# Attention, SoLU and softplus layers in one kernel: outputs of the split pairs made turned round, a TensorE subtraction for eight pairs, and a new order

## The chip, the cores and the metric

The kernel runs on one core of a Trainium2 chip. The metric is the time of one execution on the device in microseconds (us); the median of three runs of the kernel before is 711.85 us, from 709.94 to 712.74. A core has a TensorE for matmuls (PE in the profile, its weight loads PEld), VectorE (DVE), ScalarE (ACT), GpSimd (POOL) and SyncE (SP), which issues the DMAs; each engine works through its own list in order, and semaphores tie the lists together.

## The reference

Windowed attention (32 keys for the first four heads; every fourth of 128 for the last four), a layer with SoLU and layer norm, and a layer with softplus. Batch 4, 8 heads, 576 tokens, head size 64; 2304 tokens of 512 features for what follows.

```python
scores = scale * np.matmul(q, k.transpose(0, 1, 3, 2))
scores = np.where(masks[None, :, :, :], scores, -1000000000.0)
scores = scores - np.max(scores, axis=-1, keepdims=True)
attn = np.exp(scores)
attn = attn / (np.sum(attn, axis=-1, keepdims=True) + 1e-09)
x = np.matmul(attn, v)            # then tokens by 512 features

h = x @ w_in                      # 512 -> 1024
e = np.exp(h - np.max(h, axis=-1, keepdims=True))
solu = h * e / (np.sum(e, axis=-1, keepdims=True) + 1e-09)
mu = np.mean(solu, axis=-1, keepdims=True)
var = np.mean((solu - mu) ** 2, axis=-1, keepdims=True)
y = ((solu - mu) / np.sqrt(var + 1e-06) * g_ln) @ w_out     # 1024 -> 512

h2 = y @ w2_in                    # 512 -> 2048
g = np.maximum(h2, 0.0) + np.log1p(np.exp(-np.abs(h2)))
out = g @ w2_out                  # 2048 -> 512
```

## The kernel before

Large products are made from fp16 numbers: every fp32 operand is split into a high half and a low half (what the high half left over), and three products (high by high, high by low, low by high) add up in the accumulator. So each operand costs a conversion (high) and a subtraction (low).

**Attention.** Seven pairs of blocks for each batch, 28 in all; a block is 80 or 96 query rows, four heads, and 80 to 128 keys. The first ten pairs run in whole fp32 (`pair32`, `block32`), since TensorE has time early on. The other 18 (`pair`, `block`, line 1205) run on fp16 halves, and these 36 blocks are what the change is about. One of them goes like this: eight score matmuls; a masked maximum on VectorE; the exponential on ScalarE; the conversion to the high half `p` and the subtraction for the low half; a DMA that turns both over into `pT`; twelve matmuls of probabilities times values (`values`, line 1242), with `pT` as the stationary operand and 65 columns of `v` moving, of which the 65th is ones and yields the softmax sum. Then VectorE adds the epsilon to the sum, inverts it, scales the outputs into `xf` (or ScalarE does), splits these into `x`, and a DMA turns them over into `xr`, a ring of 768 tokens that holds the first layer's operand. The dilated heads go by way of `xd` and a reordering copy on ScalarE.

**Layers.** `m1` is the first layer's first product, for 18 tiles of 128 tokens (matmuls `ps_w<-W,xr`); `y` its second (`bank<-lnT,W`). The second layer goes in nine groups of 256 tokens: `h` (`bank<-y,W`), softplus, and `o` (`ps_w<-W,g`). The weights are scaled and split on VectorE and ScalarE as well, the second layer's in four quarters of its hidden width; the first two groups follow quarter by quarter as the weights come. `s1i` is the scale of the first weight, which needs the whole of it loaded.

**Order.** All work is first listed in a plan (class `Plan`, line 63) with an estimated cost for each engine that may do it. `order` (line 149) plays the plan through as events: each engine takes the ready piece that is due earliest, where the due times are the numbers of `TABLE` in tenths of a microsecond, one for each piece. Where TensorE has nothing in that play before 400 us, a filler is put into its list (line 263): a matmul of an identity matrix by itself into a free bank, 512 columns (`bank<-eye`, `ps_w<-eye`), whose result nobody reads. The list is fixed when the kernel is built. On the chip every engine runs its list in that order, and fillers run whether TensorE would have been idle or not. All recorded operations carry the lines of small helpers: 654 for a matmul, 660 for a TensorE transpose, 636 for ScalarE, 640, 642, 645, 648, 651 and 672 for VectorE, 663 and 666 for DMAs.

Of the kernel before, what the change touches and what calls it, by code (L numbers as in the profile page):

```python
# [20 lines left out]
DIL = 4  # L21
# [44 lines left out]
class Plan:  # L66
# [50 lines left out]

    def pace(self, now, us, cols):

        per = cols / us  # L120
        while True:
            w = int(now / self.WIN + 1e-9)
            while len(self.acts) <= w + 1:
                self.acts.append(0.0)
                self.fast.append(False)
            if w and not self.known[-1] >= w:
                for x in range(self.known[-1] + 1, w + 1):
                    self.fast[x] = self.acts[x - 1] >= self.KEEP
                    self.known.append(x)
            speed = 1.0 if self.fast[w] else 0.5  # L130
            left = (w + 1) * self.WIN - now
# [5 lines left out]
            now = (w + 1) * self.WIN  # L137
# [11 lines left out]
    def order(self):  # L149
# [18 lines left out]
        self.acts, self.fast, self.known, self.dense = [0.0], [False], [0], []  # L168
# [6 lines left out]
        while events:  # L175
# [120 lines left out]
def kernel(  # L296
# [35 lines left out]
    XL_PE = 0  # L332
# [640 lines left out]
    def pair(n):  # L973
# [62 lines left out]
        def vpart(s):  # L1036
            return v2.t[:kr, s, :, 0:D]
# [605 lines left out]
```

## Time and profile before

| | |
|---|---|
| median of three runs | 711.85 us |
| profiled execution, its own time | 712.54 us |
| its span in the trace | 710.8 us |
| mean granted TensorE clock | 0.983 of full speed |
| TensorE busy | 688.7 us, 97% |
| VectorE busy | 512.8 us, 72% |
| ScalarE busy | 440.1 us, 62% |
| DMA moved | 89.82 MB |

Busy shares are averages over stretches that differ. The kernel has a front, in which weights are converted and attention begins, and a long remainder of products; which engine is full has to be read for each stretch. The time from one group's start to the next one's start on TensorE says what a group costs there, since matmuls overlap and their recorded durations hold a pipeline's length.

### The profile page before, as it was taken

The numbers are of one execution on the slowest core, as the hardware profiler recorded it, in microseconds if no ns is written. First come the engines' busy times: TensorE is split into PE (matmuls) and PEld (weight loads), VectorE is DVE, ScalarE is ACT, GpSimd is POOL, SyncE is SP. The second block draws the span as 40 slices with busy tenths as digits, with TensorE's granted clock in tenths as the row PEclk, the third lists the DMA queues.
The fourth block names the chain that finished last, engine by engine and source line by source line (L and its number), as shares of the span: only waits on it lengthen the run. The fifth ranks groups of instructions, "written<-read, shape, count | busy, mean of one in ns | idle before, by whom it ended". The sixth has DMA issues, their size and how long they took to land.

```text
span 710.8 us, 14269 instructions
## 1 busy us (share of the span) xinstructions
PE 688.7 (97%) x5319; PEld 474.9 (67%) x5319; DVE 512.8 (72%) x1562; ACT 440.1 (62%) x909; POOL 3.5 (0%) x22
## 2 busy tenths in 40 slices
PE   6999797999999999999999999999999999999997
PEld 3665554867765577777765767677765677578853
DVE  4699999999999959958989989989555214411032
ACT  5588998889999478767787768749353102011110
POOL 1000000000000000000000000000000000000000
PEclk9799889999999999999999999999999999999999
DMA  9977886479966458979787786543110003000001
GB/s 265 243 210 232 260 229 174 134 159 194 226 115 149 138 165 198 237 134 166 143 163 133 136 166 124 109 93 71 42 35 26 1 1 90 1 1 1 1 30 60
DMA packets 186774, 89.82 MB, mean 126 GB/s; under 512 B 157000, under 2 KB 174416, under 8 KB 186704
## 3 DMA queue, kind: packets, MB, share of 16 engines
q1 hardware_dynamic: 186704, 88.90, 54.0%
q8 instruction: 42, 0.69, 0.4%
q14 instruction: 28, 0.23, 0.1%
HBM read 54.53 MB, written 4.72 MB: 83 GB/s over the span
## 4 chain that ended last, share of the span: by engine, by line
PE 70%; DVE 19%; DMA 4%; ACT 4%; issue 2%; SPq 0%; DVEq 0%; ACTq 0%
PE bank L654 37%; PE ps_w L654 32%; DVE W L645 3%; DVE E L645 2%; DVE st L1349 2%; DMA rk<-in_k_dram 1%; DVE s L1223 1%; DMA pT<-p 1%; DVE e L645 1%; DVE st L645 1%; PE bank L660 1%; DMA E<-in_k_dram 1%; DVE xr L648 1%; DVE hl L648 1%; ACT hl L636 1%
## 5 line engine op out<-in xcount | busy, mean ns | idle before, releaser
L654 PEld LDWEIGHTS <-W 128*128 128x128 f16 x2592 | 252.1, 98 | 36.6 <-issue 1.0
L654 PE MATMUL bank<-y,W 128*128 128x256 f16 x1728 | 196.2, 273 | 0.0
L654 PE MATMUL ps_w<-W,g 128*128 128x512 f16 x864 | 194.3, 379 | 0.0
L654 PEld LDWEIGHTS <-g 128*128 128x128 f16 x864 | 83.5, 98 | 92.0
L636 ACT ACTIVATE r<-bank,invC 128x512 f32<-128x512 f32 x72 | 49.0, 685 | 110.4 <-PE bank L654 79.6
L654 PE MATMUL ps_w<-W,xr 128*128 128x512 f16 x432 | 99.0, 382 | 0.1
L654 PE MATMUL bank<-lnT,W 128*128 128x256 f16 x864 | 97.4, 273 | 0.4 <-ACT r L636 0.4
L640 DVE TENSOR_SCALAR g<-r,KR 128x512 f16<-128x512 f32 x49 | 23.7, 484 | 86.9 <-PE ps_w L654 86.1
L654 PEld LDWEIGHTS <-xr 128*128 128x128 f16 x432 | 41.9, 100 | 46.9 <-issue 1.8
L645 DVE SCALAR_TENSOR_TENSOR g<-r,KR,g 128x512 f16<-128x512 f32 x72 | 53.8, 748 | 18.7 <-ACT g L636 15.4
L1611 ACT ACT_TABLE_LOAD x51 | 65.4, 1283 | 0.9
L636 ACT ACTIVATE s<-s 96x128 f32<-96x128 f32 (+3 forms) x144 | 43.7, 375 | 15.6 <-DVE s L642 9.3
L636 ACT ACTIVATE E<-E 128x768 f32<-128x768 f32 (+3 forms) x55 | 39.9, 729 | 13.3 <-DMA E<-in_v_dram 6.0
L1223 DVE CUSTOM_DVE_ANT_0 s<-bank,band,bsc 96x128 f32<-96x128 f32 (+3 forms) x144 | 39.0, 325 | 2.2 <-PE bank L654 1.2
L636 ACT ACTIVATE e<-ps_w,st,bsc 128x1024 f32<-128x1024 f32 x16 | 19.3, 1203 | 20.0 <-DVE st L640 14.5
L636 ACT ACTIVATE y<-bank 128x512 f16<-128x512 f32 x15 | 8.9, 591 | 33.7 <-PE bank L654 33.7
L645 DVE SCALAR_TENSOR_TENSOR E<-E 128x512 int32<-128x512 int32 x42 | 27.7, 684 | 0.0
L645 DVE SCALAR_TENSOR_TENSOR y<-bank,y 128x512 f16<-128x512 f32 x18 | 12.3, 686 | 21.3 <-ACT y L636 21.2
L1349 DVE TENSOR_REDUCE st<-ps_w 128x1 f32<-128x1024 f32 x18 | 22.0, 1222 | 7.8 <-PE ps_w L654 7.8
L654 PEld LDWEIGHTS <-eye 128*128 128x128 bf16 (+2 forms) x162 | 16.7, 110 | 14.5 <-issue 5.8
L654 PEld LDWEIGHTS <-pT 128*96 128x96 f16 (+3 forms) x432 | 22.6, 123 | 4.6 <-issue 1.0
L636 ACT ACTIVATE xf<-bank,rs 80x64 f32<-80x64 f32 (+1 forms) x92 | 21.0, 315 | 6.0 <-DVE rs L651 5.8
(197 smaller groups left out, 883.2 us busy)
## 6 DMA issues: line engine op xcount, KB each, us to landing
E<-in_moe_w_out_dram SPq DMA_DIRECT2D x18, 512.0 KB, 4.4
E<-in_moe_w_in_dram SPq DMA_DIRECT2D x16, 512.0 KB, 6.0
out_dram<-osb SPq DMA_DIRECT2D x18, 256.0 KB, 2.4
W<-in_moe_w_in_dram SPq DMA_DIRECT2D x8, 512.0 KB, 6.3
E<-in_v_dram SPq DMA_DIRECT2D x9, 384.0 KB, 4.2
E<-in_q_dram SPq DMA_DIRECT2D x9, 384.0 KB, 3.6
E<-in_k_dram SPq DMA_DIRECT2D x9, 384.0 KB, 4.0
W<-in_moe_w_out_dram SPq DMA_DIRECT2D x6, 512.0 KB, 5.4
```

The costliest lines, as they stand in the source:

```text
L636: pin(nc.scalar.activation(out=out, in_=in_, func=func, **kw))
L640: pin(nc.vector.tensor_scalar(out=out, in0=in0, scalar1=s1, scalar2=None, op0=op0))
L645: pin(nc.vector.scalar_tensor_tensor(out=out, in0=in0, scalar=s, in1=in1, op0=op0, op1=op1, **kw))
L648: pin(nc.vector.tensor_tensor(out=out, in0=a, in1=b, op=op))
L654: pin(nc.tensor.matmul(out, l, r, start=start, stop=stop))
L660: pin(nc.tensor.transpose(out, in_, eye32[:in_.shape[0], :in_.shape[0]]))
L1223: pin(nc.vector.tensor_tensor_reduce(out=sv()[:rows, h, :nk], in0=sb.t[:rows, h, :nk], in1=band[:rows, 48 - m:48 - m + nk], scale=sc[:rows ...
L1349: ({"DVE": (1.142, 0.14)}, lambda e: pin(nc.vector.tensor_reduce(out=col(0), in_=ph(), axis=AXX, op=ALU.max, negate=True)), [mb], [ps]),
L1611: pin(nc.scalar.preload_act_table_set(TABLES[tab]))
```

## The change

In `block`, the softmax sum now comes from the exponential itself (`accum_out`), and the probabilities are divided by it before they are split. The twelve matmuls swap their operands: 64 columns of `v` are stationary and the 80 or 96 rows of `pT` move, so that the outputs come out turned, feature by token. Two heads share a bank: the even one writes output partitions 0 to 63, the odd one 64 to 127, and the two alternate (`for g in range(2)`). High and low halves are then written straight into the ring, which takes away `xf` and `x` of these blocks, 36 turning DMAs, `xd`'s part and the reordering copies. The matmuls now wait for the ring's place (`wait`).

In `block32`, the low halves of the first eight pairs are made by TensorE: a matmul by a negative identity (`neg`) subtracts the high half in the accumulator (`xp`), and a copy takes the rest; before, VectorE subtracted.

The planner gets other constants (the windows by which it expects TensorE's speed, the price of a filler), some more orderings between pieces, and a new `TABLE`.

```diff
-    WIN, KEEP, HOLD = 3.4133, 3.0, 3.2
+    WIN, KEEP, HOLD = 3.4133, 3.25, 3.2
...
+    COLD = 10.0
...
+    def warm(self, w):
+        a = self.acts
+        return w >= 3 and a[w - 2] + a[w - 1] >= self.KEEP and a[w - 3] + a[w - 2] >= self.KEEP
...
-                idle_at["PE"] = self.pace(now, *self.FILL)
-                self.dense.append((now, idle_at["PE"], self.FILL[1]))
+                w = int(2 * now / self.WIN + 1e-9)
+                self.acts.extend([0.0] * (w + 2 - len(self.acts)))
+                self.acts[w] += self.FILL[1]
+                idle_at["PE"] = now + self.FILL[0] * (2 if now < self.COLD else 1)
...
-    XL_PE = 0
+    PV_US = 0.34
+    XL_PE = 8
...
     TABLE = (
-        170, 331, 228, 367, 475, 421, 396, 566, 185, 248, 154, 525, 248, 201, 208, 209, 237, 282, 204, 176, 278,
...
-    x2_pool = pool("x2", 1, [128, 2, HH, D], FP16)
-    xd_pool = Pool("xd", [])
...
-        if XL_PE:
+        if n < XL_PE:
             def residue(e):
                 for c0, cnt, r0, step in spans:
                     add(xt()[:, :, c0:c0 + cnt], neg, ring(0, r0, cnt, step))
...
-                act(sv()[:rows, h, :nk], sv()[:rows, h, :nk], ACTF.Exp, bias=nm()[:rows, h:h + 1])
+                act(sv()[:rows, h, :nk], sv()[:rows, h, :nk], ACTF.Exp, bias=nm()[:rows, h:h + 1], accum_out=mx()[:rows, h:h + 1])
...
-            for h in range(HH):
-                for x, (a, c) in enumerate(((0, 0), (0, 1), (1, 0))):
-                    mm(px[:rows, h, :], ptb.t[:nk, a * HH + h, :rows], v2.t[:nk, c, at[h], :], x == 0, x == 2)
-
-        pv = P.op(f"PV{name}", pe_cost(0.47), values, cols=0.6, after=[pt, *v_ops, *pv_ops[-1:]], uses=[ptb, v2, xb])
...
+            else:
+                tt(sv()[:rows, :, :nk], sv()[:rows, :, :nk], nm()[:rows].unsqueeze(2).broadcast_to([rows, HH, nk]), ALU.mult)
...
+            (TINY, lambda e: ts(nm()[:rows], mx()[:rows], 2.0 ** -14, 1e-9, ALU.mult, ALU.add)),
+            ({"DVE": (0.115, 0.14)}, lambda e: recip(nm()[:rows], nm()[:rows])),
+            ({**dve_cost(HH * nk), **act_cost(nk, ptr=1, k=4)}, times),
...
+            for c in range(2):
+                for x, (a, w) in enumerate(((0, 0), (1, 0), (0, 1))):
+                    for g in range(2):
+                        h = 2 * c + g
+                        mm(xt()[D * g:D * g + D, c, :rows], v2.t[:nk, w, at[h], :], ptb.t[:nk, a * HH + h, :rows], x == 0, x == 2)
+
+        pv = P.op(f"PV{name}", pe_cost(PV_US), values, cols=12e-3 * rows, after=[pt, *v_ops, *wait, *pv_ops[-1:]], uses=[ptb, v2, xb])
...
+                cast(e, ring(0, r0, cnt, step), xt()[:, :, c0:c0 + cnt], 2.0 ** -14)
...
+                stt(ring(1, r0, cnt, step), xt()[:, :, c0:c0 + cnt], 2.0 ** -14, ring(0, r0, cnt, step), ALU.mult, ALU.subtract)
```

**TensorE, the end of one block of probabilities times values before the last weight quarter.** In the kernel before (`pT` turned probabilities, `v` values, `xr` the ring):

```order
L654 LDWEIGHTS pT_105
L654 MATMUL bank_137<-v_111,pT_105 96x65
L654 LDWEIGHTS pT_105
L654 MATMUL bank_137<-v_111,pT_105 96x65
L654 LDWEIGHTS xr
L654 MATMUL ps_w_140<-W,xr 128x512
L654 LDWEIGHTS xr
L654 MATMUL ps_w_140<-W,xr 128x512
```

And in the changed kernel, at the corresponding place:

```order
L658 MATMUL bank_128<-pT_97,v_103 64x96
L658 LDWEIGHTS v_103
L658 MATMUL bank_128<-pT_97,v_103 64x96
L658 LDWEIGHTS v_103
L658 MATMUL bank_128<-pT_97,v_103 64x96
L658 LDWEIGHTS eye
L658 MATMUL bank_129<-eye 128x512
L658 LDWEIGHTS eye
```

`v` has become the stationary operand, and behind the block stand ten fillers (`eye`) where the first layer's matmuls followed.

**SP, the loads of the first weight.** Before (`W<-in_moe_w_in_dram` and `E<-in_moe_w_in_dram` are its pieces, eight in all; the last row here is the eighth):

```order
L663 DMA E<-in_moe_w_in_dram 128x1024 x2
L663 DMA W<-in_k_dram 128x4x64
L663 DMA W<-in_moe_w_in_dram 128x1024
L663 DMA W<-in_q_dram 96x4x64
L663 DMA W<-in_moe_w_in_dram 128x1024
```

Now, the rows that end with the eighth piece:

```order
L671 DMA W<-in_q_dram 96x4x64
L671 DMA W<-in_moe_w_out_dram 128x1024
L671 DMA rk_100<-in_k_dram 128x4x64
L671 DMA e_108<-in_moe_g_ln_dram 8x128
L671 DMA xd<-in_v_dram 128x4x64
L671 DMA rk_100<-in_k_dram 128x4x64
L671 DMA W<-in_k_dram 112x4x128
L671 DMA E<-in_moe_w_out_dram 128x1024
L671 DMA qk<-in_v_dram 128x4x64
L671 DMA E<-in_moe_w_out_dram 128x1024
L671 DMA xd<-in_v_dram 128x4x64
L671 DMA W<-in_moe_w_in_dram 128x1024
```

The eighth piece moved behind further loads of q, k and v, `g_ln`, and three pieces of `w_out`.

**VectorE, the middle of a split block.** Before (`s` scores and probabilities, `rs` the inverted sum, `xf` outputs, `x` their halves):

```order
L642 TENSOR_SCALAR s_113<-s_113 96x4
L640 TENSOR_SCALAR rs_166<-bank_137 96x4
L651 RECIPROCAL rs_166<-rs_166 96x4
L648 TENSOR_TENSOR xf_115<-bank_137,rs_166 96x256
L672 CAST x_116<-xf_115 96x256
L648 TENSOR_TENSOR x_116<-xf_115,x_116 96x256
```

Now (with weight conversions `E` and outputs `osb` between):

```order
L655 RECIPROCAL s_105<-s_105 96x4
L649 SCALAR_TENSOR_TENSOR E<-E 128x512
L649 SCALAR_TENSOR_TENSOR osb_123<-ps_w_131,invD,osb_123 128x512
L649 SCALAR_TENSOR_TENSOR osb_124<-ps_w_131,invD,osb_124 128x512
L680 CAST p_106<-s_104 96x512
L652 TENSOR_TENSOR s_105<-s_105 96x512
L652 TENSOR_TENSOR p_106<-s_104,p_106 96x512
L649 SCALAR_TENSOR_TENSOR xr<-bank_128,xr 128x2x72
```

The normalisation moved from the outputs to the probabilities, ahead of the split (`p`), and the ring's low half is made straight from the accumulator.

## Rows read from the trace of the kernel before

**Rows 1.** Windows: columns from to, length, busy (x instructions) of each engine, clock, DMA.
```profile
0.00:40.00 40.00, 33.38 (x216) 20.50 (x216) 24.24 (x63) 21.88 (x68) 3.52 (x22) 0.87 0.92 258
80.00:100.00 20.00, 16.72 (x97) 11.08 (x98) 19.46 (x47) 19.82 (x58) 0.00 (x0) 0.66 0.97 259
137.00:229.00 92.00, 91.65 (x737) 64.17 (x735) 91.36 (x291) 86.18 (x176) 0.00 (x0) 1.00 0.83 173
251.00:706.00 455.00, 453.40 (x3565) 318.86 (x3563) 280.69 (x875) 230.25 (x393) 0.00 (x0) 1.00 0.42 89
```

**Rows 2.** Timeline of TensorE around 136 us: start, length in us, operation.
```profile
135.17 0.82 PE L654 MATMUL bank<-qk,pT 128*96 128x65 f32 x8
135.82 1.24 PE L654 MATMUL ps_w<-eye 128*128 128x512 bf16 x5
136.90 1.36 PE L654 MATMUL bank<-y,W 128*128 128x256 f16 x11
```

**Rows 3.** Waits of TensorE from 136.9 us on: total, times, longest.
```profile
PE bank L654 <- ACT r L636: 0.4, 1, 0.4
...
PE bank L654 <- DMA pT<-p: 0.2, 1, 0.2
...
PE bank L654 <- DVE s L1223: 0.2, 1, 0.2
```

**Rows 4.** Timeline of TensorE around 245 us.
```profile
239.74 0.59 PE L654 MATMUL bank<-eye 128*128 128x512 bf16 x2
...
240.17 2.75 PE L654 MATMUL ps_w<-W,xr 128*128 128x512 f16 x12
...
245.49 5.40 PE L654 MATMUL bank<-y,W 128*128 128x256 f16 x48
...
250.73 0.38 PE L654 MATMUL bank<-eye 128*128 128x512 bf16 x1
```

**Rows 5.** Groups of VectorE by form: count, busy, mean ns, idle before.
```profile
L645 DVE SCALAR_TENSOR_TENSOR W<-W 128x512 int32<-128x512 int32 x22 | 15.1, 689 | 0.2
...
L645 DVE SCALAR_TENSOR_TENSOR W<-W,s2i 128x512 f16<-128x512 f32 x8 | 5.8, 744 | 0.0
...
L648 DVE TENSOR_TENSOR xr<-bank,xr 128x144 f16<-128x144 f32 x8 | 3.8, 474 | 0.6 <-ACT xr L636 0.5
...
L648 DVE TENSOR_TENSOR xr<-bank,xr 128x192 f16<-128x192 f32 x8 | 2.8, 352 | 0.2 <-ACT xr L636 0.2
```

**Rows 6.** DMA issues by kind, timeline of SP, and timeline of VectorE.
```profile
W<-in_moe_w_in_dram SPq DMA_DIRECT2D x8, 512.0 KB, 6.3
...
17.92 0.33 SPq L663 DMA_DIRECT2D W<-in_moe_w_in_dram  x1
...
39.75 0.15 DVE L640 TENSOR_SCALAR s1i<-tmp 128x1 f32<-128x1 f32 x1
```

**Rows 7.** Timeline of TensorE at two blocks.
```profile
181.79 0.69 PE L654 MATMUL bank<-v,pT 128*96 128x65 f16 x12
...
182.32 5.41 PE L654 MATMUL bank<-y,W 128*128 128x256 f16 x48
...
187.56 0.62 PE L654 MATMUL bank<-v,pT 112*80 112x65 f16 x12
...
188.01 0.57 PE L654 MATMUL bank<-kT,qT 128*80 128x112 f16 x8
...
188.47 1.80 PE L654 MATMUL bank<-y,W 128*128 128x256 f16 x15
```

**Rows 8.** Timeline of TensorE at an fp32 pair.
```profile
69.40 1.00 PE L654 MATMUL bank<-kT,qT 64*80 64x112 f32 x16
70.32 0.50 PE L660 MATMUL bank<-eye,rq 80*128 80x80 f32 x4
```

**Rows 9.** Groups of VectorE by form.
```profile
L648 DVE TENSOR_TENSOR p<-s,p 96x512 f16<-96x512 f32 x14 | 9.6, 683 | 0.1
...
L651 DVE RECIPROCAL rs<-rs 96x4 f32<-96x4 f32 x24 | 4.1, 169 | 0.1
```

More of the change, by code (lines that the diff above doesn't have):

```diff
@@ L116, in shy @@
         return self.SHY if e == "DVE" and len(o.opts) > 1 else 0.0
+    def warm(self, w):
+        a = self.acts
+        return w >= 3 and a[w - 2] + a[w - 1] >= self.KEEP and a[w - 3] + a[w - 2] >= self.KEEP
     def pace(self, now, us, cols):
         per = cols / us
+        part = self.WIN / 2
         while True:
-            w = int(now / self.WIN + 1e-9)
+            w = int(now / part + 1e-9)
             while len(self.acts) <= w + 1:
                 self.acts.append(0.0)
[L125 to L131, printed above, removed]
+            speed = 1.0 if self.warm(w) else 0.5
+            left = (w + 1) * part - now
             if us <= left * speed + 1e-9:
@@ L136, in pace @@
             us -= left * speed
-            now = (w + 1) * self.WIN
+            now = (w + 1) * part
     def short(self, now):
@@ L527 @@
     ams = [mem([128, 9], FP32, f"am{b}") for b in range(B)]
-    amw = [mem([128, 8], FP32, f"amw{i}") for i in range(2 + 2 * NQ)]
+    amw_mem = mem([128, 16 + 8 * NQ], FP32, "amw")
+    amw = [amw_mem[:, 0:8], amw_mem[:, 8:16], *(amw_mem[:, 16 + 4 * i:20 + 4 * i] for i in range(2 * NQ))]
     tmp = [mem([128, 8], FP32, f"tmp{i}") for i in range(4)]
@@ L589 @@
     xf_pool = pool("xf", 1, [128, HH, D], FP32)
-    x2_pool = pool("x2", 1, [128, 2, HH, D], FP16)
-    xd_pool = Pool("xd", [])
-    xd_pool.add(xd_mem.bitcast(FP16).rearrange("p (c r i) -> p c r i", c=4, r=DIL), opens=late)
-    dg_pool = pool("dg", 2 if LO_PE else 0, [128, 128], FP32)
+    dg_pool = Pool("dg", [quarter(3, 1152 + 128 * i, 128) for i in range(4)] if LO_PE else [])
     e_pool = pool("e", 1, [128, F1], FP32)
@@ L657, in add, with turned @@
         pin(nc.tensor.matmul(out, l, r, start=False, stop=True, skip_group_check=True))
-    def turned(out, in_):
-        pin(nc.tensor.transpose(out, in_, eye32[:in_.shape[0], :in_.shape[0]]))
+    def turned(out, in_, start=True):
+        one = eye32[:in_.shape[0], :in_.shape[0]]
+        if start:
+            pin(nc.tensor.transpose(out, in_, one))
+        else:
+            pin(nc.tensor.matmul(out, in_, one, is_transpose=True, start=False, stop=True, skip_group_check=True))
     def dma(out, in_):
@@ L724 @@
         nc.gpsimd.memset(s[0], 0.0)
-    for s in v_pool.slots:
-        nc.gpsimd.memset(s[0][:, 0, :, D:D + 1], 1.0)
-        nc.gpsimd.memset(s[0][:, 1, :, D:D + 1], 0.0)
     gb, gp = Buf(e_pool), Buf(ps_x)
@@ L1055, in pair, with landing @@
         )
-        x2s = []
         for o in range(2):
             at = [2 * h + o if kind else HH * o + h for h in range(HH)]
-            block(n, o, kind, b, i, half, rows, m[o], nk[o], sc, qt, kt, v2, at, [q_t, k_t], [v_h, v_l], due, x2s)
+            block(n, o, kind, b, i, half, rows, m[o], nk[o], sc, qt, kt, v2, at, [q_t, k_t], [v_h, v_l], due)
+    def landing(kind, b, i, o, half):
+        if kind == 0:
+            t0 = b * S + (2 * i + o) * RP
+            return [(0, RP, t0 % RING, 1)], token_wait(t0, t0 + RP), None
+        u = 2 * b + half
+        t0 = u * UNIT
+        off = (RD - UNIT // DIL) * half
+        spans, at = [], 0
+        while at < UNIT:
+            r0 = (t0 + at) % RING
+            cnt = min(UNIT - at, RING - r0)
+            spans.append((off + at // DIL, cnt // DIL, r0 + 2 * i + o, DIL))
+            at += cnt
+        return spans, token_wait(t0, t0 + UNIT), u
     def pair32(n, b, kind, i, half, rows, kr, m, nk, bufs, lds, due):
@@ L1095, in scores @@
                     mm(scored(o)[:rows, h, :nk[o]], qt.t[part, h, :rows], kt.t[part, h, :nk[o]], False, h == HH - 1)
-        qk_mm = P.op(f"QK{n}", pe_cost(0.05 + (4 + PAIRED * 16) * sum(nk) / 2400), scores, cols=4e-3 * sum(nk), after=turns, uses=[qt, kt, *sbs])
+        qk_mm = P.op(f"QK{n}", pe_cost(0.05 + (4 + PAIRED * 16) * sum(nk) / 2400), scores, cols=12e-3 * sum(nk), after=[*turns, *qk_ops[-1:]], uses=[qt, kt, *sbs])
+        qk_ops.append(qk_mm)
         for o in range(2):
@@ L1126, in block32 @@
         )
[L1127 to L1141 removed]
+        spans, wait, u = landing(kind, b, i, o, half)
         val = slice(1 - o, UW - o)
@@ L1148, in values @@
                 mm(px()[:rows, h, :], ptb.t[:nk, h, :rows], v3.t[:nk, h, UW * o:UW * (o + 1)], True, True)
-        pv = P.op(f"PV{name}", pe_cost(0.56), values, after=[cp, *v_ops, *wait, batch_ok[b]], uses=[ptb, v3, xb])
+        pv = P.op(f"PV{name}", pe_cost(0.56), values, cols=8e-3 * UW, after=[cp, *v_ops, *wait, batch_ok[b]], uses=[ptb, v3, xb])
         last32.append(pv)
@@ L1203, in block32, with block @@
             x_done.setdefault(u, []).append(xl)
-    def block(n, o, kind, b, i, half, rows, m, nk, sc, qt, kt, v2, at, qk_ops, v_ops, due, x2s):
+    def block(n, o, kind, b, i, half, rows, m, nk, sc, qt, kt, v2, at, turned_ops, v_ops, due):
         name = f"{n}.{o}"
         sb, s2, pb, ptb, xb = Buf(ps_s), Buf(s_pool), Buf(p_pool), Buf(pT_pool), Buf(ps_x)
-        xfb, x2b = Buf(xf_pool), Buf(x2_pool)
-        x2s.append(x2b)
         def scores(e):
@@ L1262, in block @@
-            ({"DVE": (0.115, 0.14)}, lambda e: recip(rr[:rows], rr[:rows])),
-            ({**dve_cost(256, x=1), **act_cost(64, ptr=1, psum=1, k=4)}, times, [], [xfb]),
-        ], after=[pv], uses=[xb])
-        xv = lambda: xfb.t
-        x_h = P.op(f"xh{name}", either(256), lambda e: cast(e, x2b.t[:rows, 0], xv()[:rows]), after=[nr], uses=[xfb, x2b])
-        x_l = P.op(f"xl{name}", dve_cost(256), lambda e: tt(x2b.t[:rows, 1], xv()[:rows], x2b.t[:rows, 0], ALU.subtract), after=[x_h], uses=[xfb, x2b])
@@ new lines, in block, with values @@
+        pt = P.op(f"pT{name}", dma_cost(1.35, 1.8), lambda e: dma_t(ptb.t[:, :, :rows], pb.t[:rows].rearrange("p a h c -> p (a h c)")), after=[p_l], uses=[pb, ptb], mv=moving(8 * rows, 256, 1.8))
+        spans, wait, u = landing(kind, b, i, o, half)
+        xt = lambda: xb.t[:, 0:2 * RP].rearrange("p (c r) -> p c r", c=2)
+        def values(e):
+            for c in range(2):
[3 more added lines that the diff above has]
+                        mm(xt()[D * g:D * g + D, c, :rows], v2.t[:nk, w, at[h], :], ptb.t[:nk, a * HH + h, :rows], x == 0, x == 2)
@@ new lines, in block, with ring, high, low @@
+        pv = P.op(f"PV{name}", pe_cost(PV_US), values, cols=12e-3 * rows, after=[pt, *v_ops, *wait, *pv_ops[-1:]], uses=[ptb, v2, xb])
+        pv_ops.append(pv)
+        def ring(a, r0, cnt, step):
+            return xr[:, kind, 2 * a:2 * a + 2, r0:r0 + (cnt - 1) * step + 1:step]
+        def high(e):
+            for c0, cnt, r0, step in spans:
+                cast(e, ring(0, r0, cnt, step), xt()[:, :, c0:c0 + cnt], 2.0 ** -14)
+        def low(e):
+            for c0, cnt, r0, step in spans:
+                stt(ring(1, r0, cnt, step), xt()[:, :, c0:c0 + cnt], 2.0 ** -14, ring(0, r0, cnt, step), ALU.mult, ALU.subtract)
@@ L1305 @@
+        k = len(spans)
+        n_x = 2 * sum(x[1] for x in spans) / k
+        xh = P.op(f"xh{name}", {**act_cost(n_x, psum=1, k=k), **dve_cost(n_x, x=1, k=k)}, high, after=[pv], uses=[xb])
+        xl = P.op(f"xl{name}", dve_cost(n_x, x=1, k=k), low, after=[xh], uses=[xb], due=due)
+        if kind == 0:
+            x_done[b, 0, 2 * i + o] = [xl]
+        else:
+            x_done.setdefault(u, []).append(xl)
     ln_bufs = {}
@@ L1464, in mlp2 @@
         add_prev = [None, None]
+        g_prev = g_last[-1] if not early else None
         for p in range(NP):
```

108 lines of the change are left out of this document (30 added, 78 removed), and 285 rows, old and new, of the table TABLE.

## Prediction

> **What bounds the kernel now.** I read the windows first, for which engine fills which stretch. VectorE is filled early: 19.46 of the 20 us from 80, in which TensorE's granted clock is 0.66 of full speed (the mean of its two levels, 1.2 and 2.4 GHz), and 91.36 of the 92 us from 137 to 229 [rows 1]. TensorE takes over when the second MLP can start: its first `h` matmuls begin at 136.90, right behind five filler matmuls [rows 2], and from there TensorE is busy 91.65 of the 92 us up to 229 and 453.40 of the 455 from 251 [rows 1]. The waits after 136.9 are five, 1.5 us in sum, the longest 0.4, the shortest 0.2 [rows 3]. So two clocks rule: before 137 us what VectorE must finish before the first `h`, after it how long TensorE's list is, fillers included. Third, the stretch to the last weight quarter: its first `h` is at 245.49 and the last filler at 250.73 [rows 4].
>
> The sum is made against the profiled execution, 712.54 us (span 710.8 and 1.74 around it), which is 0.7 above the median of 711.85.
>
> **First term: the start of the second MLP.** The second low half of `y` on VectorE is the gate of the first `h`. I counted VectorE's instructions up to it in both orders: 331 before, 313 after. The heavy ones that leave are four W<-W,s2i (744 ns each) and four W<-W (689) that now come later or go to ScalarE, and the subtractions that made the fp32 pairs' low halves: eight of 144 columns (474) and six of 192 (352) [rows 5], 11.6 us in sum; smaller ones (single conversions, 96-column subtractions, scale steps) make some 4 more. What is new ahead of it is near 11 us: weight conversions moved forward and to VectorE, four normalisations of outputs more, one pass over 1024 columns. Counted from an instruction's start to the next one's start, about 0.07 us less than its duration, the balance is 115.7 against 111.9: −3.8 us. VectorE is full there, so I take all of it: the first `h` at 133.1.
>
> Against it stands the load of the first weight. Its eighth piece is issued at 17.92 us and such pieces land after some 6 us [rows 6]; in the new order it stands twelve rows further back in SP's queue, with 9.6 MB ahead of it in place of 6.7. At 258 GB/s of the first 40 us [rows 1] that is 37 us in place of about 25, and its scale, at 39.75 now [rows 6], may be 3 to 5 us late. VectorE has other rows to do meanwhile (the count above holds them), so I charge nothing; uncovered it costs up to 5. Bounds of this term: −10 (VectorE's waits in the slow-clock stretch go as well) and +2.
>
> The 18 `xp` matmuls of the new low halves (two spans for some pairs) stand in this front, where TensorE waits for VectorE anyway; by the price of a filler each, 0.216 us, they are at most 3.9 us and cost nothing while VectorE sets the pace. ScalarE gets their copies, the sums of 144 exponentials and part of the normalising, and loses the six reordering copies and about half of the output scalings: some +9 us over the run, in an engine that is busy 86.18 of 92 us up to 229, without holding TensorE there, and 230.25 of 455 from 251 [rows 1].
>
> **Second term: fillers.** TensorE's list holds 142 fillers before and 217 after. Ahead of the first `h` there are 139 and 179; these lie under VectorE's work. Between the first `h` and the last quarter's first `h` it was 2 and is 38, with one more behind it before and none after: 35 more. Price: two fillers from 239.74 to 240.17, 0.216 us each [rows 4], so 7.6 us of TensorE's full list. A filler that stands where TensorE would wait is free; the five waits of 1.5 us in all [rows 3] show that about 0.8 of it may be: +6.8. Bounds: 0 (all stand where TensorE is held for the weights of the last quarter, VectorE's work for which has grown from 226.6 to 229.0 us by the same count), and +7.6.
>
> **Third term: probabilities times values.** 36 blocks of 12 matmuls. Before, 65 columns move: 20 blocks of 80 rows take 0.45 us (187.56 to 188.01), 16 of 96 rows 0.53 (181.79 to 182.32) [rows 7], 17.5 us in all. Now 80 or 96 columns move, with 64 columns stationary, alternately into the upper and the lower output partitions. If the halves run one behind the other, a column costs what the scores cost: eight matmuls of 112 columns in 0.46 us (188.01 to 188.47) [rows 7], 0.51 ns a column, so 0.49 and 0.59 us a block, 19.3 us: +1.8. If they run side by side, half of that, 9.7: −7.8. The trace has such a pair, though on row halves: sixteen records of fp32 score matmuls of 112 columns on 64 rows take from 69.40 to 70.32, 57 ns each, 0.51 ns a column, where eight records of 65 columns on whole rows take 0.65 us (135.17 to 135.82), 1.25 a column [rows 2, 8]. So row halves overlap. I take half the serial time and 0.1 us a block for entering and leaving the form, a choice between the ends that no row gives: 13.3 us, −4.2. Column halves aren't shown by any row, so both ends stay in the range.
>
> The row shows the half form running more than twice as fast per column. The Trainium skill, page "TensorEngine Tiling (Array Packing)", section "Key Properties", says that tiles work in parallel but that changing the tiling mode drains TensorE; the drain speaks against 36 blocks that each enter and leave the mode, and would be paid 72 times. No row here has the drain alone. The same skill's page "TensorE: Matmul & The Clock Gate", section "LDWEIGHTS (loading the stationary operand)", puts a load at its columns divided by 1.2 ns; by it 12 loads of 64 columns would alone take 0.64 us a block, an estimate, and the term would be +5.5. The trace disagrees with that as a spacing: load and matmul of 80 stationary columns follow each other every 38 ns [rows 7], where the rule gives 67.
>
> **The chain of a block.** Between exponential and fp16 split now stand a scalar step, a reciprocal (169 ns) and a multiplication over 512 columns, for which the nearest row is the p<-s,p subtraction, 683 ns [rows 9]: 1.0 us longer before the transposing DMA, and the single `p` buffer stays the same. Behind the matmuls the chain gets shorter: two steps to the ring in place of five steps and a DMA. VectorE's load per block is even. I take no wait from it, since chains run a block or more ahead and TensorE waited once, 0.2 us, for pT [rows 3]. SP loses 36 transposes; the queue isn't what is waited for after 41 us.
>
> Sum: −3.8 + 6.8 − 4.2 = −1.2 on 712.54, 711.3; less 0.7 for the median, 710.6 us.
>
> **Rivals.** (A) Faster: the halves overlap without a switching cost (−7.8 in place of −4.2) and the fillers keep the clock up where it stood at 0.66 for 20 us, 6.8 us of full speed [rows 1], so that the first `h` comes at about 127 (−10). With all fillers priced: 712.5 − 10 − 7.8 + 6.8 − 0.7 = 700.8; half of the front's gain gives 704. For it: TensorE's matmuls feed VectorE in that stretch. Against: VectorE has no idle time there to give back.
> (B) Slower: the longer chain arrives late at TensorE. The new list puts 9, 14 and 10 fillers right around blocks of probabilities times values: the order itself foresees TensorE without work there. Each block that isn't covered costs its 1.0 us; as queued work on TensorE stands behind the block in a fixed order, nothing fills it. It decides from five late blocks on (715.6); with eight, 710.6 + 8 = 718.6. For it: VectorE is full to 229, so each of the added steps queues. Against: 28 of the 36 blocks come after the last filler, where VectorE is busy 280.69 of 455 us [rows 1].
> (C) The change doesn't do what it says: the halves go serially, +1.8 in place of −4.2, and the time is 716.6.
>
> **Chances.** The forecast 0.5 (706 to 715), A 0.18, B 0.2, C 0.12. The measurement tells 0.5% from no change, that is below 708.3 or above 715.4. Of the forecast's half 0.15 lies below, 0.3 between, 0.05 above; A is below but for 0.02; B is above but for 0.04; C is split 0.04 to 0.08. Faster 0.31, same 0.40, slower 0.29. The range that leaves out a tenth on either side is 701 to 720.
>
> **What would show it.** The first `h` at 133 (right) or past 137 (load of the first weight or chain late). The blocks' slots on TensorE: 0.34 and 0.40 us if the halves overlap with a cost around them, 0.25 and 0.3 without, 0.5 and 0.6 if serial. The last quarter's first `h` within 3 us of 245.5 and TensorE busy over 99% behind it; waits on pT, or on a ring copy, of more than 3 us in sum speak for B. Wrong in principle would be a TensorE that waits after 260 us, or fillers that take over 0.3 us each because the clock is low.

## The result, and the profile after

The changed kernel takes 716.7 us (median) against 711.51 for the kernel before in the same comparison, a ratio of 1.0066 with an interval from 1.004 to 1.0092: slower by about 5 us. I had forecast 710.6 and a range up to 720; the time lies in the range, on the wrong side of the kernel before. One of its six executions took 1851.61 us, stands outside the ratio, and without it the median is 716.6. The profiled execution took 716.6 us, span 714.9, mean clock 0.994.

The windows of the changed kernel (from to, length, busy time of PE, PEld, DVE, ACT and POOL, clock, DMA share, GB/s), to hold against [rows 1]:

```profile
0.00:40.00 40.00, 34.81 (x267) 21.47 (x268) 25.81 (x62) 26.35 (x81) 3.37 (x18) 1.00 0.98 276
80.00:100.00 20.00, 15.92 (x109) 9.93 (x107) 19.35 (x57) 19.06 (x53) 0.00 (x0) 0.83 0.80 221
133.00:229.00 96.00, 94.00 (x743) 63.92 (x742) 93.64 (x293) 85.72 (x195) 0.00 (x0) 1.00 0.71 161
257.00:710.00 453.00, 451.94 (x3564) 311.69 (x3563) 275.65 (x854) 241.98 (x518) 0.00 (x0) 1.00 0.40 83
```

The clock is full over the first 40 us (0.87 before) and 0.83 in place of 0.66 from 80 to 100, and TensorE is busy nearly everywhere. A reader of these four lines would see a kernel that got better. Where the second layer begins on TensorE (start, length, operation), against [rows 2]:

```profile
131.74 0.60 PE L658 MATMUL ps_w<-eye 128*128 128x512 bf16 x2
132.17 1.55 PE L658 MATMUL bank<-qk,pT 96*96 96x65 f32 x16
133.56 2.78 PE L658 MATMUL bank<-y,W 128*128 128x256 f16 x24
```

The first `h` is at 133.56, 3.3 us earlier. Two blocks of probabilities times values, against [rows 7]; the next row's start ends the slot:

```profile
187.27 0.45 PE L658 MATMUL bank<-pT,v 128*64 128x96 f16 x12
187.65 0.61 PE L658 MATMUL bank<-y,W 128*128 128x256 f16 x4
...
205.80 0.41 PE L658 MATMUL bank<-pT,v 112*64 112x80 f16 x12
206.14 2.79 PE L658 MATMUL bank<-y,W 128*128 128x256 f16 x24
```

0.38 and 0.34 us a block, where it was 0.53 and 0.45. Now TensorE ahead of the last weight quarter, against [rows 4]; the last row is the quarter's first `h`:

```profile
222.76 0.41 PE L658 MATMUL bank<-pT,v 112*64 112x80 f16 x12
223.10 2.12 PE L658 MATMUL bank<-eye 128*128 128x512 bf16 x9
226.42 2.75 PE L658 MATMUL ps_w<-W,g 128*128 128x512 f16 x12 [1.20 <-DVE osb L649]
...
234.81 3.18 PE L658 MATMUL bank<-eye 128*128 128x512 bf16 x14
237.92 0.45 PE L658 MATMUL bank<-pT,v 128*64 128x96 f16 x12
238.30 2.33 PE L658 MATMUL bank<-eye 128*128 128x512 bf16 x10
240.65 7.93 PE L658 MATMUL ps_w<-W,xr 128*128 128x512 f16 x36
248.42 0.28 PE L658 MATMUL bank<-amw,ones 128*128 128x4 f32 x2
248.56 2.75 PE L658 MATMUL ps_w<-W,xr 128*128 128x512 f16 x12
251.15 0.59 PE L658 MATMUL bank<-eye 128*128 128x512 bf16 x2
251.58 0.60 PE L658 MATMUL bank<-y,W 128*128 128x256 f16 x4
```

It is at 251.58, 6.1 us later than before, behind 33 fillers in three places and two more just ahead of it. In that list `bank<-amw,ones` at 248.42 is the matmul that sums the squares of the last weight piece: the second weight's scale, without which the quarter's `h` is not let go in the plan. VectorE's steps from it to the scale, in the changed kernel:

```profile
248.74 0.16 DVE L846 TENSOR_REDUCE tmp<-bank 128x1 f32<-128x4 f32 x1 [1.17 <-PE bank L658]
248.93 0.15 DVE L644 TENSOR_SCALAR s2o<-tmp 128x1 f32<-128x1 f32 x1
...
250.79 0.15 DVE L649 SCALAR_TENSOR_TENSOR KR<-s2o,tmp 128x1 f32<-128x1 f32 x1
```

and the same steps in the kernel before:

```profile
243.08 0.16 DVE L840 TENSOR_REDUCE tmp<-bank 128x1 f32<-128x4 f32 x1 [0.16 <-PE bank L654]
243.28 0.15 DVE L640 TENSOR_SCALAR s2o<-tmp 128x1 f32<-128x1 f32 x1
...
245.02 0.15 DVE L645 SCALAR_TENSOR_TENSOR KR<-s2o,tmp 128x1 f32<-128x1 f32 x1
```

The scale is 5.7 us later, and in both kernels `h` starts within a us of `KR`. That does not make the scale what TensorE waits for: its matmul stands in TensorE's own list, straight behind 36 matmuls of the first layer, VectorE waits 1.17 us for it (0.16 before), and `h` follows behind twelve more matmuls and two fillers without a pause. The scale marks how late the stretch is. The account of the span, +4.1: first `h` −3.3; from there to the last quarter's first `h` 118.0 us in place of 108.6, +9.4; from there to the last matmul 458.1 in place of 459.9, −1.8; the tail −0.2.

The windows of the stretch that got longer, from the first `h` to the last quarter's, before and then now:

```profile
136.90:245.50 108.60, 108.25 (x824) 72.05 (x823) 107.04 (x339) 94.58 (x190) 0.00 (x0) 1.00 0.76 166
133.56:251.60 118.04, 116.02 (x863) 73.78 (x863) 113.11 (x352) 96.14 (x216) 0.00 (x0) 1.00 0.64 150
```

VectorE is 6.1 us busier in it (113.11 in place of 107.04) and idle for 3.4 us more (4.9 in place of 1.6): together the 9.4.

### The profile page after: what moved, and what is told of

The parts are those of the page before. It is cut to its first block, busy times and chain, and to the rows that moved or that the text cites. A ratio compares the mean times of both kernels' runs of the same rounds, so it can differ in the third digit from the quotient of the medians.

```text
span 714.9 us, 14467 instructions
## 1 busy us (share of the span) xinstructions
PE 696.0 (97%) x5412; PEld 468.9 (66%) x5412; DVE 511.7 (72%) x1536; ACT 452.5 (63%) x1056; POOL 3.4 (0%) x18
## 4 chain that ended last, share of the span: by engine, by line
PE 72%; DVE 12%; DMA 7%; ACT 6%; issue 2%; SPq 0%; DVEq 0%; ACTq 0%
PE bank L658 37%; PE ps_w L658 33%; DMA E<-in_moe_w_in_dram 2%; DMA lnT<-hl 2%; DVE E L649 2%; PE bank L666 2%; ACT E L640 1%; DVE W L649 1%; DMA pT<-p 1%; ACT W L640 1%; DVE s L1230 1%; DMA E<-in_moe_w_out_dram 1%; ACT hl L640 1%; ACT e L640 1%; DMA rk<-in_k_dram 1%
## 5 line engine op out<-in xcount | busy, mean ns | idle before, releaser
L658 PEld LDWEIGHTS <-W 128*128 128x128 f16 x2592 | 251.6, 98 | 35.4 <-issue 0.4
L640 ACT ACTIVATE s<-s 96x128 f32<-96x128 f32 (+3 forms) x156 | 57.4, 375 | 14.4 <-DVE s L646 12.1
L640 ACT ACTIVATE E<-E 128x768 f32<-128x768 f32 (+3 forms) x51 | 38.0, 745 | 16.4 <-DVE E L649 9.4
L1230 DVE CUSTOM_DVE_ANT_0 s<-bank,band,bsc 96x128 f32<-96x128 f32 (+3 forms) x144 | 39.0, 324 | 13.0 <-PE bank L658 12.8
L658 PEld LDWEIGHTS <-eye 128*128 128x128 bf16 (+2 forms) x237 | 23.1, 104 | 23.0 <-POOL eye L721 3.8
L640 ACT ACTIVATE xr<-bank 128x144 f16<-128x144 f32 (+2 forms) x76 | 26.8, 402 | 16.9 <-PE bank L658 14.0
L658 PE MATMUL ps_w<-eye 128*128 128x512 bf16 x131 | 36.1, 396 | 0.2 <-DVE e L649 0.2
L640 ACT ACTIVATION_READ_ACCUMULATOR s<-s 80x1 f32 (+1 forms) x144 | 26.9, 187 | 0.0
```

The costliest lines, as they stand in the source:

```text
L640: pin(nc.scalar.activation(out=out, in_=in_, func=func, **kw))
L658: pin(nc.tensor.matmul(out, l, r, start=start, stop=stop))
L1230: pin(nc.vector.tensor_tensor_reduce(out=sv()[:rows, h, :nk], in0=sb.t[:rows, h, :nk], in1=band[:rows, 48 - m:48 - m + nk], scale=sc[:rows ...
```

## The experiments

Theory 1: the fillers fill TensorE's list and cost their price. Theory 2: VectorE reaches the last scale later, TensorE must wait for it, and the fillers only stand in the wait. Beside it a question of the second kind: what the short blocks are due to. Times below are medians, with the ratio to the kernel before measured on the same chip and its interval; the starts are read from each run's timeline. The starts come from one profiled execution of each run and scatter by 1 to 1.5 us: experiment 3 only reorders the twelve matmuls of a block and has the last quarter at 250.6 where the changed kernel has 251.6, and experiment 1 changes nothing ahead of the first `h` and has it at 135.0 where the changed kernel has 133.6. The table holds, in us, the first `h`, the scale steps (`s2o<-tmp`) and the first `h` of the last quarter, and the stretch from there to the last matmul.

| run | first h | last scale | last quarter | behind it | ratio (interval) |
|---|---|---|---|---|---|
| before | 136.9 | 243.3 | 245.5 | 459.9 | 1 |
| changed | 133.6 | 248.9 | 251.6 | 458.1 | 1.0066 (1.004 to 1.0092) |
| 1, no late fillers | 135.0 | 253.6 | 255.8 | 457.2 | 1.0115 (1.0093 to 1.0136) |
| 2, no multiplication | 133.7 | 247.2 | 249.8 | 457.4 | 1.0047 (1.0027 to 1.0067) |
| 3, halves in turn | 133.7 | 248.0 | 250.6 | 459.1 | 1.0069 (1.0044 to 1.0093) |
| 4, multiplication on ScalarE | 133.0 | 249.3 | 252.0 | 459.2 | 1.0093 (1.0072 to 1.0115) |
| 8, low halves on VectorE | 135.5 | 249.8 | 252.5 | 456.8 | 1.007 (1.0048 to 1.0092) |
| 13, no block work early | 133.4 | 246.3 | 248.9 | 457.1 | 1.0035 (1.0017 to 1.0054) |
| 14, no sums early | 133.9 | 247.9 | 250.5 | 458.3 | 1.0057 (1.0037 to 1.0076) |
| 15, before, more on VectorE | 135.7 | 246.8 | 249.0 | 459.7 | 1.0064 (1.0036 to 1.0093) |

**1. The late fillers left out.**

```diff
+        late_part = late_part or isinstance(o, Op) and o.name == "h0.0"
+        if late_part and not isinstance(o, Op):
+            continue
```

Expected: 

> The changed kernel without the 38 fillers that stand after the first h matmul; the order of everything else is kept. Theory 1 (the fillers fill TensorE's list and cost their 0.216 us each): 8.2 us less, 708 to 709. Theory 2 (VectorE reaches the scale of the last weight quarter 5.7 us later, TensorE has to wait for it, and the fillers stand in that wait): the first h of the last quarter stays near 251, waits of 8 to 10 us appear in its place, and the time is 715 to 717.5.

Measured: 719.76 us, 3 us slower than with them. TensorE in the same stretch (idle time and its releaser in brackets), and the windows:

```profile
223.60 0.41 PE L658 MATMUL bank<-pT,v 112*64 112x80 f16 x12
226.71 4.44 PE L658 MATMUL ps_w<-W,g 128*128 128x512 f16 x12 [2.70 <-DVE osb L649]
...
239.79 0.45 PE L658 MATMUL bank<-pT,v 128*64 128x96 f16 x12 [2.85 <-DVE xr L649]
242.63 10.61 PE L658 MATMUL ps_w<-W,xr 128*128 128x512 f16 x36 [2.39 <-DVE osb L649]
```

```profile
220.00:240.00 20.00, 14.45 (x89) 6.55 (x89) 17.46 (x42) 10.05 (x27) 0.00 (x0) 0.91 0.40 104
240.00:260.00 20.00, 17.61 (x100) 9.47 (x95) 15.25 (x47) 10.67 (x21) 0.00 (x0) 0.83 0.41 132
```

Waits stand in the fillers' three places, 7.9 us in sum, for VectorE's output sums (`osb`) and a low half of the ring (`xr`). The granted clock falls there: the twelve matmuls behind the first wait take 4.44 us in place of 2.75, the 36 of the first layer behind the third 10.61 in place of 7.93. The last quarter starts 4.2 us later still, of which 1.4 is there at the first `h` already. Theory 1 falls: without the fillers TensorE waits in their place, and with them it keeps the clock. Theory 2 had waits of the right size, on the right engine and in the fillers' places, but not what is waited for, which is never the scale; and it missed the clock, 2 us above its range.

**2. The multiplication left out.**

```diff
-        o.fn(o.on)
+        if not (o.name.startswith("nr") and o.name.endswith("c") and int(o.name[2:].split(".")[0]) >= NF):
+            o.fn(o.on)
```

Expected: 

> The changed kernel with the multiplication of the probabilities by the inverted sum left out in the 36 split blocks (sum and reciprocal stay), so the outputs are not divided by the softmax sum; order kept, fillers too. Theory 1: TensorE's list is as long as before, 716 to 717. Theory 2: five of these passes (0.57 us each from start to start) leave VectorE ahead of the last quarter's scale, and the blocks' chains get shorter; the scale and the first h of the last quarter come 2 to 4 us earlier, 712.5 to 714.5.

Measured: 714.95 us. The last quarter starts 1.8 us earlier and the time is 1.8 lower. The direction is theory 2's, the size just short of what it had; but by experiment 3's trace the quarter is only 0.8 us earlier, and the intervals of the ratios overlap, so a gain is likely and not certain.

**3. Halves in turn.**

```diff
-                for x, (a, w) in enumerate(((0, 0), (1, 0), (0, 1))):
-                    for g in range(2):
-                        h = 2 * c + g
+                for g in range(2):
+                    h = 2 * c + g
+                    for x, (a, w) in enumerate(((0, 0), (1, 0), (0, 1))):
```

Expected: 

> The changed kernel with the twelve matmuls of a split block in the order head by head (three into the upper output half, then three into the lower) in place of alternating. If the alternation is what lets them run side by side, a block takes 0.49 and 0.59 us in place of 0.34 and 0.38; the 28 blocks behind the last quarter's start cost 5 us, 721 to 722 us. If the alternation doesn't matter, 716 to 717.5.

Measured: 716.48 us, ratio 1.0069 (1.0044 to 1.0093). The alternation does not matter; a miss for the first reading. Whether the short slots are real was then open, hence 5 to 7.

**4. Five multiplications on ScalarE.**

```diff
+        if isinstance(o, Op) and o.name in ("nr10.0c", "nr11.1c", "nr12.0c", "nr13.0c", "nr13.1c"):
+            o.on = "ACT"
```

Expected: 

> The changed kernel with five of the multiplications ahead of the last weight quarter's scale (blocks 10.0, 11.1, 12.0, 13.0, 13.1) on ScalarE in place of VectorE, same place in the order. Theory 1: no change, 716 to 717. Theory 2: VectorE is 2.9 us earlier at that scale, 713.5 to 715, unless ScalarE's four instructions for each (about 1.6 us) make the block's chain late, which would take part of it back.

Measured: 718.13 us; the last scale did not come earlier (249.3), and the remainder got 1.1 us longer. The remainder of experiment 3 is as long without such a cause (459.1), so the 1.1 is scatter. VectorE's relief was lost on ScalarE, which is 18.7 to 19.8 us busy of each 20 from 180 to 220 in the changed kernel: VectorE waits for it 4.7 us between 133 and 252 us, 0.6 in the changed kernel. So the proviso held, in full.

**5 to 7. Each block's matmuls five times**, in the changed kernel alternating, head by head, and in the kernel before.

```diff
+            for again in range(5):
                 for c in range(2):
                     for x, (a, w) in enumerate(((0, 0), (1, 0), (0, 1))):
```

Expected, alternating: 

> The changed kernel with the twelve matmuls of each split block issued five times over (the same result each time), halves alternating. If the slots in the trace (0.34 and 0.38 us) are what TensorE is held for, the four extra passes cost 4 x 0.35 us in each of the 28 blocks behind the last quarter's start, 39 us, and up to 51 with the eight ahead of it: 756 to 768. If the matmuls really take a column's time of the scores, 0.49 and 0.59, it is 60 to 77 us: 777 to 794.

Expected, head by head: 

> The same five passes, but head by head (three matmuls into the upper output half, then three into the lower). If a side-by-side run of the halves makes the short slots, it needs alternation, and this comes out 15 to 25 us above the alternating one. If the 64 columns of the stationary operand make them, the two are within 2 us.

Expected, the kernel before: 

> The kernel before with its twelve matmuls of each split block issued five times over. By its slots (0.45 and 0.53 us) the extra passes cost 4 x 0.49 us in 28 to 36 blocks, 55 to 71 us: 767 to 782. The difference to the alternating run of the changed kernel, per pass and block, is what the new form saves.

Measured: 746.85, 746.81 and 779.48 us, two executions of each. The 144 extra passes cost 30 us in either new form, 0.21 a pass, and 68 us in the old, 0.47. The new form came out below both of my numbers, since the first pass of a block is dearer than the next four (and of the 33.5 us by which the blocks' slots grew, some fell into TensorE's waits). The new form's timeline:

```profile
175.32 1.47 PE L658 MATMUL bank<-pT,v 128*64 128x96 f16 x60
176.72 0.50 PE L658 MATMUL bank<-y,W 128*128 128x256 f16 x3
```

and the old form's:

```profile
189.91 2.46 PE L654 MATMUL bank<-v,pT 112*80 112x65 f16 x60
192.20 0.57 PE L654 MATMUL bank<-kT,qT 128*80 128x112 f16 x8
```

Five passes of 96 columns take 1.40 us (175.32 to 176.72) where one takes 0.38: 0.255 for each further one, 21 ns a matmul, 0.22 ns a column, under half of the scores' 0.51 [rows 7]. So the short slots are real. Head by head is as fast, which by the expectation of that run speaks for the 64 stationary columns as the reason, and not for halves that need alternation. Whether two halves run side by side is not shown: no run puts all twelve matmuls into one half. Five passes of 80 columns take 1.20 us in the same trace, 0.215 for each further one. A block alone thus costs 0.12 us more than a further pass, of its 0.34 or 0.38; I put that down to entering and leaving the form. In the old form five passes take 2.29 us (189.91 to 192.20), 0.46 each, the first no dearer than the others.

**8. The low halves of the first eight pairs on VectorE again.**

```diff
-                    add(xt()[:, :, c0:c0 + cnt], neg, ring(0, r0, cnt, step))
+                return
...
-                    cast(e, ring(1, r0, cnt, step), xt()[:, :, c0:c0 + cnt])
+                    tt(ring(1, r0, cnt, step), xt()[:, :, c0:c0 + cnt], ring(0, r0, cnt, step), ALU.subtract)
```

Expected: 

> The changed kernel with the low halves of the first eight pairs subtracted on VectorE from the accumulator again, at the places where the copies stood, and without the 18 subtracting matmuls; all else in the same order. If VectorE's list sets the first h and the last quarter's scale, its 15 to 18 more instructions (0.27 to 0.4 us each) put both 4 to 5 us later, 719.5 to 721. If the front has slack, 716 to 717.5.

Measured: 716.75 us, no change that the intervals resolve. The first `h` is 1.9 us later, little more than the scatter, the last scale 0.9, and nothing of it is seen at the end. This part of the change is worth nothing that these runs can tell.

**9 to 11. The last two quarters' weight work pulled ahead in the built order**, by up to 6 and 3 us, and by 6 in the kernel before.

```diff
+    for x in [o for o in order if isinstance(o, Op) and o.name.startswith(("w2i2", "w2o2", "w2i3", "w2o3")) and o.on != "SP"]:
+        at = order.index(x)
+        to = at
+        while to and not clash(x, order[to - 1]) and (not isinstance(order[to - 1], Op) or order[to - 1].t0 > x.t0 - 6.0):
+            to -= 1
+        order.insert(to, order.pop(at))
```

Expected, 6 us: 

> The changed kernel with every instruction of the second layer's last two weight quarters (their conversions, squares, scales on VectorE, ScalarE and TensorE) pulled ahead of other work in the built order by up to 6 us of the plan, as far as what it reads and writes allows; nothing added or left out. Theory 2a (the place of these instructions in VectorE's list sets the last quarter's start): the scale and the first h of the last quarter come 3 to 5 us earlier, 712 to 714. Theory 2b (loads, squares and the scale matmul set it, VectorE waits then at these places): no change, 716 to 717.5, with VectorE's waits grown by as much. Theory 2c (the work pushed behind makes the blocks and o late): the quarter starts earlier, but TensorE waits elsewhere, 716 to 719.

Expected, 3 us: 

> As the one before, but pulled ahead by up to 3 us only. 2a: 1.5 to 3 us earlier, 714 to 715.5. 2b: no change. 2c: less of a delay elsewhere than with 6, 715.5 to 717.

Expected, the kernel before: 

> The kernel before with the same pull of up to 6 us. In it TensorE's list is full up to the last quarter's start (waits and fillers of 1 us there), so an earlier scale can give at most 1 us: 710.5 to 712; if the blocks are made late, 713 to 715.

Measured: 767.67, 742.86 and 761.82 us, 51, 26 and 50 us slower (the third against the kernel before): none of my theories had that. What VectorE waits for from 137 to 300 us in the first of them (total, times, longest):

```profile
DVE tmp L846 <- PE bank L658: 11.7, 4, 4.8
DVE E L646 <- DMA E<-in_moe_w_out_dram: 8.0, 3, 3.9
DVE st L1339 <- PE ps_w L658: 6.3, 1, 6.3
DVE E L646 <- DMA E<-in_moe_w_in_dram: 5.5, 3, 2.5
```

Pulled ahead, an instruction stands at the head of an in-order list before its load or its matmul is there, and all behind it wait. The chain to the scale is thus load, conversion, square, matmul, each on another engine with two load buffers, and VectorE's list is full in between: a chain and a full engine at once.

**12. `h` without the second weight's scale.**

```diff
-            need = [*w2_d[qd][0], w2_ok[qd]]
+            need = w2_d[qd][0]
...
-                lambda e, ps=ps, rb=rb, cq=cq: act(rb.t, ps.t, ACTF.Softplus, scale=invC[:, cq]), after=[hm], uses=[ps, rb], tab=2,
+                lambda e, ps=ps, rb=rb, cq=cq: act(rb.t, ps.t, ACTF.Softplus, scale=invC[:, cq]), after=[hm, *scaled_by], uses=[ps, rb], tab=2,
```

Expected: 

> The changed kernel in which a quarter's h matmuls wait for that quarter's first weight alone, and only the softplus behind them for the scale of the second weight (which is what it reads); the planner makes a new order from that. If the wait for the scale is what TensorE loses, h of the last quarter starts some 12 us earlier and up to two of them run ahead of the scale: 5 us less, 711.5 to 713. If other work is missing then in the same place (the first layer's tiles), 715 to 718.

Measured: 715.0 us, ratio 1.006 (1.0038 to 1.0082). The last quarter's first `h` moved to 234.6, the scale stayed at 250.6, and 26 fillers now stand in one row ahead of `y`: two `h` run ahead, then TensorE is without work again. The ratio is that of the changed kernel (1.006 and 1.0066): no gain, though `h` no longer stands behind the scale. The planner made a new order for it, so more than this differs.

**13 to 15. Less VectorE work, fewer ScalarE sums, and more VectorE work in the kernel before**, each in the pairs 10 to 13, which come ahead of the last quarter. 13 leaves out their normalising steps and low halves, 14 the sums.

```diff
+        if o.name.startswith(("nr10", "nr11", "nr12", "nr13", "xl10", "xl11", "xl12", "xl13")):
+            continue
```

```diff
-                act(sv()[:rows, h, :nk], sv()[:rows, h, :nk], ACTF.Exp, bias=nm()[:rows, h:h + 1], accum_out=mx()[:rows, h:h + 1])
+                act(sv()[:rows, h, :nk], sv()[:rows, h, :nk], ACTF.Exp, bias=nm()[:rows, h:h + 1], **({} if n < 14 else {"accum_out": mx()[:rows, h:h + 1]}))
...
-            (TINY, lambda e: ts(nm()[:rows], mx()[:rows], 2.0 ** -14, 1e-9, ALU.mult, ALU.add)),
+            (TINY, lambda e: ts(nm()[:rows], mx()[:rows], *((0.0, 1.0) if n < 14 else (2.0 ** -14, 1e-9)), ALU.mult, ALU.add)),
```

```diff
         o.fn(o.on)
+        if o.name.startswith(("pl10", "pl11", "pl12", "pl13")):
+            o.fn(o.on)
```

Expected, 13: 

> The changed kernel in which the four split pairs that come ahead of the last quarter's start (10 to 13) leave out VectorE's normalising steps (scalar step, reciprocal, multiplication) and the low half into the ring; three multiplications of ScalarE go too. Order and fillers kept. Some 7 us of VectorE's list ahead of the last scale. If VectorE's block work is the cause: the last scale 4 to 6 us earlier, near the 243 us of the kernel before, and the total 711 to 713. If loads or ScalarE set it: 715 to 717.

Expected, 14: 

> The changed kernel in which the exponentials of the pairs 10 to 13 don't read out their sums (32 of them, about 0.1 us of ScalarE each; the outputs of these pairs are not divided by the sum). If ScalarE sets the last quarter's start: 2 to 3 us earlier, 713.5 to 715. If VectorE does: 716 to 717.5.

Expected, 15: 

> The kernel before with the low half of the probabilities of the pairs 10 to 13 made twice (8 more passes of about 0.57 us on VectorE, same result), order kept. If VectorE's list ahead of the last scale is the bound: the scale and the last quarter's start 3 to 4.6 us later and the total 714.5 to 716.5, as in the changed kernel. If VectorE has slack there: 711 to 712.5.

Measured: 713.62, 715.75 and 715.44 us. The mirror, 15, came out as theory 2 had it: eight more passes, some 4.6 us of VectorE, put the last quarter of the kernel before 3.5 us later (4.8 counted from its first `h`) and the time 4 us up. 13 gives 2.7 us at the last quarter (1.7 by experiment 3's trace) and 3 in the time, less than I had expected. Its window from the first `h` to the last quarter says why:

```profile
133.40:248.90 115.50, 115.50 (x862) 73.77 (x862) 108.06 (x323) 92.81 (x204) 0.00 (x0) 1.00 0.66 154
```

VectorE has 5.0 us less to do than in the changed kernel, and TensorE is not idle for a moment. The fillers were kept, 38 in 8.5 us of this stretch, and with VectorE relieved they are the limit: more than TensorE's 2.0 us of idle time (118.04 less 116.02) could hardly be gained in 2, 13 or 14. 13 without fillers was not run.

14 has the last quarter at 250.5, which is where experiment 3 has it (250.6), and its ratio can't be told from the changed kernel's. No effect of ScalarE's sums is shown.

## Why the prediction was wrong

- First term, the first `h` 3.8 us earlier: right (3.3). The count of VectorE's instructions carried it. The late load of the first weight also came (`s1i` at 45.35 in place of 39.75) and was hidden, as charged. But I let this gain count to the end. Part of it was work put off: four `W<-W,s2i`, which the count takes out ahead of the first `h`, start between 133.97 and 138.55 now, 3.0 us of VectorE right behind it (rows below). Experiment 8 points the same way: 1.9 us lost ahead of the first `h` left nothing in the time that the intervals resolve.
- Third term, the blocks: the size was right, 17.7 us of slots down to 12.8, −4.9 where I had −4.2, and the cost around a block is 0.12 us, I had 0.1. The reason, halves side by side like the fp32 row halves, is not shown (5, 6). The prediction's other price, +5.5 if load time sets the spacing, is refuted by experiment 5, at 18 to 21 ns for a load and its matmul. Behind the last quarter's start, where TensorE is full, 28 blocks gave 3.8 us, of which 1.8 is left: from start to start, `h` and `o` take 1.7 and 0.8 us more there, in waits of at most 0.41.
- Second term, the fillers at +6.8: the step that failed, and with it "the last quarter's first `h` within 3 us of 245.5". I priced the fillers as added work on a full list, took that list for what bounds the stretch, and put TensorE's wait for VectorE at nothing. Experiment 1 shows the wait: without the fillers TensorE stands idle for 7.9 us in their three places, for `osb` and `xr`, and the quarter comes no earlier. The stretch is 9.4 us longer, as much as VectorE's 6.1 us of work and 3.4 of idle time more in it. That the two sums were not far apart hid the mistake: 6.8 of list against 9.4 of waiting. The price of a filler was fair, and where VectorE is relieved (13) the list with its fillers is the limit after all.
- What I should have asked is how much VectorE has to do up to the last quarter, and not only up to the first `h`. I looked at TensorE's 91.65 of 92 us in [rows 1] and called it the bound, beside VectorE's 91.36; experiment 15 shows that the stretch was bound by VectorE as much.
- "VectorE's load per block is even" and "I take no wait from it": wrong in place. Over the whole run it is even, 512.8 us of VectorE before and 511.7 after. From the first `h` to the last quarter it is not. The blocks' own steps grow by some 1.5 us there: five multiplications, eight scalar steps, eight reciprocals and the ring's low halves come in, the output steps go. Some 5 us are scalings of weight pieces, that came from ahead of the first `h` and from ScalarE. VectorE's groups in that stretch, two rows before and three now:

```profile
L640 DVE TENSOR_SCALAR W<-E,s2o 128x512 f16<-128x512 f32 x2 | 1.0, 477 | 0.0
L640 DVE TENSOR_SCALAR W<-E,s2i 128x512 f16<-128x512 f32 x1 | 0.5, 478 | 0.0
...
L649 DVE SCALAR_TENSOR_TENSOR W<-W,s2i 128x512 f16<-128x512 f32 x4 | 3.0, 742 | 0.0
L644 DVE TENSOR_SCALAR W<-E,s2o 128x512 f16<-128x512 f32 x4 | 1.8, 479 | 0.0
L644 DVE TENSOR_SCALAR W<-E,s2i 128x512 f16<-128x512 f32 x4 | 1.7, 471 | 0.0
```

- My count up to the last quarter, 226.6 to 229.0, said +2.4 us. By the windows VectorE's work up to there is 225.8 us before and 229.9 now, +4.1, with 2.0 us of idle time more: the 6.1. I had the growth as an end of the range (0 for the fillers) and not in the sum.
- Rival B had the right side, the right engine, and with the 9, 14 and 10 fillers the places of the waits. What is waited for was another thing: TensorE's waits on `pT` are 0.6 us in sum, those of experiment 1 are on `osb` and `xr`. A is out: the clock did stay higher, 0.83 in place of 0.66, and moved the first `h` no further than VectorE's list did. (Its 704 is 705.8 if half of the −10 is meant.) C is out.

Shown are: that TensorE waits for VectorE in the fillers' places (1), and that in the kernel before VectorE's list bounds this stretch as much as TensorE's (15). VectorE's block work in four pairs is worth 1.7 to 2.7 us at the last quarter (13), at most what the kept fillers let show. How the 6.1 us divide between the weight scalings and the blocks is read from the traces and not tried: no run put the scalings back. No version beat the kernel before; the nearest that leaves nothing out is 12, at 715.0.

## What to carry to other kernels

Fillers in a built order are a mark of a wait: ask what the instruction behind them waits for, and price that. They become a load only when the wait gets shorter than they are. A gain on one engine counts only up to the next point where another engine lets it go, so find these points first (here VectorE's output sums and ring halves ahead of the last quarter) and count both engines' work up to there, not only up to the start. Work that leaves one stretch has to be looked for in the next. And don't pull a critical instruction ahead in an in-order list past the time at which its inputs arrive: 3 us of it cost 26 us here.

## What the runs showed of the hardware

- Twelve matmuls with 64 stationary columns, six into each half of the output partitions, run at 18 to 21 ns each in repeated passes (0.215 us a pass for 80 moving columns, 0.255 for 96), whether the halves alternate or come three by three; a block alone takes 0.12 us more than such a pass. The whole form took 38 and 45 ns.
- TensorE idle for 2 to 3 us at a time, three times within 20 us, brought the granted clock to 0.91 and 0.83 of full speed in the windows around it; the same waits with fillers in them kept it at 1.00.
- Reading out the sum of an exponential cost ScalarE 0.09 us: from start to start 0.385 us in place of 0.293 for 96 rows of 128 columns, 0.345 in place of 0.252 for 80 rows of 80.
